# Issuing a head's four cluster-row transfers with the head's first cast instead of its fourth part

## The chip, the cores and the metric

The kernel runs on one core of one Trainium2 chip. The metric is the device time of one execution in microseconds. The core has a matrix engine (TensorE, PE in the rows), VectorE (DVE), ScalarE (ACT), GpSimd (POOL) and SyncE (SP), which here issues nearly all DMA transfers. Each engine works through its own instructions in order and waits on semaphores for the others.

## The reference

Cluster attention, a mixture of experts that sends each token to one expert, and a second dense block. The change lies in the attention:

```
mask = q_assign[:, :, :, None] == k_assign[:, :, None, :]
scores = scale * np.matmul(q, k.transpose(0, 1, 3, 2))
scores = np.where(mask, scores, -1000000000.0)
scores = scores - np.max(scores, axis=-1, keepdims=True)
attn = np.exp(scores)
attn = attn / (np.sum(attn, axis=-1, keepdims=True) + 1e-09)
return np.matmul(attn, v).astype(np.float32)
```

There are 2 x 8 = 16 heads of 768 rows and 64 columns; `q_assign` and `k_assign` are the nearest of 16 centroids by cosine.

## The kernel before, in words

Heads go in pairs `p` (0 to 7), head `h` being half of pair `h // 2`. A head has six row tiles of 128 rows, so the attention is a loop over 96 groups, `g = 6 * h + t`. The order of the instructions on every engine is the order in which the program is written (a manual schedule). One turn of the loop (L1092 to L1114) issues for group `g`: the product of the probabilities with V of an earlier head (`av_step`, L355), the scores of group `g + 2` (`S_mm`, L304 and L319), the transposes of group `g` (`P_T`, L343) with their copies out of PSUM on ACT or DVE (L348, L346), a list of side jobs, the exponential of group `g + 2` on ACT (L330), more side work listed under `after`, and one part of the preparation of a later head.

The scores are two accumulated products. L304 multiplies the tiles `qA` and `kA`, L319 adds `qB` and `kB`, whose rows 0 to 63 are the low parts of a split of q or k and whose rows 64 to 79 are the head's cluster rows: one row per centroid, so that a pair of tokens in different clusters gets a huge negative score. These 16 rows are made for a pair at once (`sims_back`, ACT L230, tile `mk`) and are brought into the operands by `put_mask`: four DMAs of 16 x 384 (24 KB each), two into `qB`, two into `kB`, all issued by SP at L295. The operand tiles have two buffers, so those of head `h` are those of head `h - 2`.

The rest of a head's operands is made by `prep_part(h, i)` in four parts, one in each of the groups `6 * h - 9` to `6 * h - 6`: part 0 a cast of k on ACT (L277), part 1 a second cast (L279) and a subtraction on DVE (L280), part 2 a scaled cast of q (L282), part 3 another (L284) and the DVE's last reading of the pair's raw q (L285). The first L319 of head `h` is issued in group `6 * h - 2`.

What shares SP's queue with L295: `load_raw` (L173 and L174, the raw q and k of a pair, 384 KB each, into two buffers, so the loading of pair `p` waits until the L285 of head `2 * p - 3` is done), `load_v` (L181), the store of finished rows (L394), and a conversion of the last block's 64-bit weights, which runs along with the attention in 16 pieces: `cv_load` (L438, 1024 KB, tile `words`), four steps on ACT and DVE of which the first is ACT's L451, and `cv_store` (L469, 512 KB).

The lines around the change:

```
h2, i2 = divmod(g - 3, NT)
h2 += 2
if 2 <= h2 < NH and i2 < 4:
    prep_part(h2, i2)
    if i2 == 3 and h2 > 2:
        put_mask(h2)
if g == 8:
    put_mask(2)
```

Of the kernel before, what the change touches and what calls it, by code (L numbers as in the profile page):

```python
# [32 lines left out]
def body(ctx, tc, qT, kT, vP, cen, mod, wg, bias, w1, w2, win, wout, out):  # L33
# [121 lines left out]
    def drain():  # L155
        while pend:
            for _ in pend.pop(0):
                pass

    def run(f, *a):  # L160

        drain()
        x = f(*a)
        if hasattr(x, "__next__"):
            next(x, None)
            pend.append(x)
# [101 lines left out]
    def prep_part(h, i):  # L268

        p, o = h // 2, 64 * (h % 2)  # L270
        if i == 0:
            spl[h] = tuple(p_sp.tile([128, S], F32R, tag=n, name=n) for n in ("qA", "kA", "qB", "kB"))
        qA, kA, qB, kB = spl[h]
        q_s, k_s = (r[o:o + 64] for r in raw[p])
        hi, lo = slice(o, o + 64), slice(64 - o, 128 - o)
        if i == 0:
            act.copy(kA[hi], k_s)  # L277
        elif i == 1:
            act.copy(kA[lo], k_s)  # L279
            dve.tensor_tensor(out=kB[0:64], in0=k_s, in1=kA[hi].bitcast(F32), op=ALU.subtract)  # L280
        elif i == 2:
            act.activation(out=qA[hi], in_=q_s, func=AF.Copy, scale=0.125)  # L282
        else:
            act.activation(out=qB[0:64], in_=q_s, func=AF.Copy, scale=0.125)  # L284
            dve.scalar_tensor_tensor(  # L285
                out=qA[lo], in0=q_s, scalar=0.125, in1=qA[hi].bitcast(F32), op0=ALU.mult, op1=ALU.subtract
            )

    def put_mask(h):
        p, i = h // 2, h % 2  # L290
        qA, kA, qB, kB = spl[h]
        for j, x in enumerate((qB, kB)):
            for a in range(2):
                o = 64 * j + 32 * a + 16 * i
                sp.dma_start(  # L295
                    out=x[64:80, a * HS:(a + 1) * HS].bitcast(F32), in_=mks[p][o:o + 16].bitcast(F32)
                )
# [11 lines left out]
    def S_mm(g):  # L309
        if g >= NH * NT:  # L310
            return
        if g not in S_t:
            S_part(g)
        h, t = divmod(g, NT)
        qA, kA, qB, kB = spl[h]
        ps = S_t[g]
        ts = slice(t * 128, t * 128 + 128)
        for i in range(2):
            pe.matmul(ps[:, i, :HS], qB[:80, ts], kB[:80, i * HS:(i + 1) * HS], start=False, stop=True)  # L319
        nm_t[g] = p_m.tile([128, 1], F32, tag="nm", name="nm", bufs=4)  # L320
        dve.tensor_reduce(out=nm_t[g], in_=ps[:, :, :HS], axis=AX.XY, op=ALU.max, negate=True)  # L321

    def S_exp(g):
        if g >= NH * NT:
            return
        h, t = divmod(g, NT)
        if t == 0:
            sums[h] = p_m.tile([128, NT], F32, tag="sums", name="sums", bufs=3)
        P_t[g] = p_P.tile([128, 2, HS], F32, tag="P", name="P")
        act.activation(  # L330
            out=P_t[g], in_=S_t.pop(g)[:, :, :HS], func=AF.Exp, bias=nm_t.pop(g), scale=1.0,
            accum_out=sums[h][:, t:t + 1],
        )

    def P_T(g):
        h, t = divmod(g, NT)
        if t == 0:
            PT[h] = p_PT.tile([128, NT, S], F32, tag="PT", name="PT")
        P = P_t.pop(g)
        for i in range(2):  # L340
            ps = ps_T.tile([128, 3, 128], F32, tag="t", name="Tp")
            for j in range(3):
                pe.transpose(ps[:, j, :], P[:, i, j * 128:(j + 1) * 128], ident)  # L343
            dst = PT[h][:, 3 * i:3 * i + 3, t * 128:(t + 1) * 128]
            if i == 0 and g not in busy:
                dve.tensor_copy(dst, ps)  # L346
            else:
                act.copy(dst, ps)  # L348
# [20 lines left out]
    def av_step(g):  # L369

        h, kt = divmod(g - NT - 1, NT)
        if kt == NT - 1:
            return
        AV(h, kt)
        if kt == NT - 2:
            AV(h, NT - 1)
            fin_av(h)
# [566 lines left out]
    with tc.manual_schedule():  # L944
# [147 lines left out]
        for g in range(NH * NT):  # L1092
            h, t = divmod(g, NT)
            if g > NT:
                av_step(g)
            S_mm(g + 2)
            P_T(g)
            for f, a in jobs.get(g, ()):
                if inspect.isgeneratorfunction(f):
                    run(f, *a)  # L1100
                else:
                    f(*a)
            S_exp(g + 2)
            drain()
            for f, a in after.get(g, ()):
                f(*a)
            h2, i2 = divmod(g - 3, NT)
            h2 += 2
            if 2 <= h2 < NH and i2 < 4:
                prep_part(h2, i2)  # L1110
                if i2 == 3 and h2 > 2:
                    put_mask(h2)
            if g == 8:
                put_mask(2)  # L1114
# [506 lines left out]
```

## Time and profile before

| what | value |
|---|---|
| median of 3 runs | 767.64 us (766.39 to 768.34) |
| the profiled execution, its own time | 767.36 us |
| its span, first to last instruction | 765.6 us |
| mean granted TensorE clock | 0.975 of full speed |
| busy over the span | PE 708.8 us (93%), DVE 450.0 (59%), ACT 416.1 (54%), POOL 128.5 (17%) |

The attention fills about the first 290 us. The times of a row are counted from the span's first instruction. A row that ends in a bracket gives the idle time of its engine just before and what ended it. "SPq" is SP's issuing queue; the time shown there is that of the issue, and the landing of a transfer is a number of its own.

### The profile page before, as it was taken

Reading aid. Unit: us, or ns where it says so; the run is one execution under the profiler, and the core shown is the slowest. Engines: PE = TensorE matmul, PEld = TensorE weight load, DVE = VectorE, ACT = ScalarE, POOL = GpSimd, SP = SyncE. Lnnn points to the kernel's source line nnn. Section 1 sums busy time; section 2 is a strip of 40 time slices with the busy share of each in tenths; the row PEclk is TensorE's granted clock in tenths of the full one; section 3 lists DMA queues with packets and bytes.
Section 4 is the critical chain, followed back from the end, with each engine's and each line's share of the span. In section 5 each row is a group of like instructions: output and inputs, shape, how many; then the busy total and the mean of one; then the engine's idle time right before and its main releaser. Section 6 shows DMA issues by size and latency. Waiting matters only on the chain. (4 is left out here: it accounts for less than half of the span.)

```text
span 765.6 us, 11692 instructions
## 1 busy us (share of the span) xinstructions
PE 708.8 (93%) x4498; PEld 564.4 (74%) x4498; DVE 450.0 (59%) x668; ACT 416.1 (54%) x663; POOL 128.5 (17%) x144
## 2 busy tenths in 40 slices
PE   4997997899798999986999999998999999999998
PEld 2764654556455555874879888997998898999887
DVE  5895987789789975863446563677143233233220
ACT  3886987798779976343446562663323323323310
POOL 4200000000310103635452522252000000000000
PEclk9898999999989999996999999999999999999999
DMA  4314454544553625979967985500010000000000
GB/s 133 105 56 174 145 198 151 171 145 160 183 131 119 199 98 167 236 110 368 355 228 277 345 301 195 179 15 20 10 42 15 28 15 15 15 1 28 1 28 27
DMA packets 38683, 99.28 MB, mean 130 GB/s; under 512 B 8255, under 2 KB 15615, under 8 KB 36577
## 3 DMA queue, kind: packets, MB, share of 16 engines
q1 hardware_dynamic: 35888, 91.42, 36.3%
q0 software_dynamic: 2592, 6.69, 2.4%
q8 instruction: 36, 0.59, 0.3%
q10 hardware_dynamic: 144, 0.39, 0.2%
q14 instruction: 23, 0.18, 0.1%
HBM read 79.13 MB, written 18.28 MB: 127 GB/s over the span
## 5 line engine op out<-in xcount | busy, mean ns | idle before, releaser
L1500 DVE SCALAR_TENSOR_TENSOR sp<-g,sp 128x1024 f32<-128x1024 f32 x24 | 29.4, 1224 | 148.8 <-ACT sp L1499 148.8
L321 DVE TENSOR_REDUCE nm<-S 128x1 f32<-128x768 f32 x96 | 90.9, 948 | 34.3 <-PE S L319 34.0
L1489 PE MATMUL g<-xh,wh 128*128 128x256 f32 x384 | 108.7, 283 | 0.0
L1489 PE MATMUL g<-xh,wl 128*128 128x256 f32 x384 | 107.9, 281 | 0.0
L1489 PE MATMUL g<-xl,wh 128*128 128x256 f32 x384 | 107.9, 281 | 0.0
L1497 ACT ACTIVATE sp<-g 128x1024 f32<-128x1024 f32 x24 | 24.6, 1027 | 136.6 <-PE g L1489 126.7
L330 ACT ACTIVATE P<-S,nm 128x768 f32<-128x768 f32 x96 | 86.9, 905 | 18.9 <-DVE nm L321 16.2
L343 PE MATMUL Tp<-ident,P 128*128 128x128 f32 x576 | 85.6, 284 | 10.7 <-ACT PT L348 7.5
L343 PEld LDWEIGHTS Tp<-ident,P 128*128 128x128 f32 x576 | 68.7, 144 | 24.5 <-ACT PT L348 14.2
L355 PE MATMUL av<-PT,v 128*64 128x384 f32 x384 | 80.7, 517 | 0.0
L741 POOL TENSOR_TENSOR wl<-raw,wh 128x1024 fp32r<-128x1024 f32 x22 | 54.1, 2469 | 139.2 <-ACT wh L740 132.2
L741 DVE TENSOR_TENSOR wl<-raw,wh 128x1024 fp32r<-128x1024 f32 x50 | 65.1, 1343 | 14.5 <-ACT wh L740 14.5
L1489 PEld LDWEIGHTS g<-xl,wh 128*128 128x128 f32 x384 | 73.0, 190 | 0.5
L740 ACT CAST wh<-raw 128x1024 fp32r<-128x1024 f32 x69 | 68.9, 1050 | 8.0 <-DMA raw<-in_w 5.4
L1489 PEld LDWEIGHTS g<-xh,wh 128*128 128x128 f32 x384 | 72.8, 190 | 0.5
L348 ACT COPY PT<-Tp 128x384 f32<-128x384 f32 x144 | 64.0, 477 | 16.8 <-PE Tp L343 16.0
L1489 PEld LDWEIGHTS g<-xh,wl 128*128 128x128 f32 x384 | 73.0, 190 | 0.0
L1524 PE MATMUL o<-wh,gT 128*128 128x512 f32 x216 | 69.7, 394 | 0.0
L319 PE MATMUL S<-kB,qB 80*128 80x384 f32 x192 | 51.8, 353 | 18.0 <-DMA kB<-mk 16.1
L843 PE MATMUL y<-wh,hT 128*128 128x512 f32 x192 | 64.7, 408 | 0.0
L304 PEld LDWEIGHTS S<-kA,qA 128*128 128x128 f32 x192 | 29.7, 194 | 47.1 <-ACT PT L348 16.2
L304 PE MATMUL S<-kA,qA 128*128 128x384 f32 x192 | 60.2, 396 | 1.2 <-ACT P L330 0.9
(284 smaller groups left out, 1396.9 us busy)
## 6 DMA issues: line engine op xcount, KB each, us to landing
raw<-in_w SPq DMA_DIRECT2D x56, 512.0 KB, 7.6
words<-in_win SPq DMA_DIRECT2D x8, 1024.0 KB, 7.4
w_rows<-cvt SPq DMA_DIRECT2D x16, 512.0 KB, 3.0
words<-in_wout SPq DMA_DIRECT2D x8, 1024.0 KB, 5.7
whole<-in_w SPq DMA_DIRECT2D x16, 512.0 KB, 6.2
raw<-w_rows SPq DMA_DIRECT2D x16, 512.0 KB, 4.6
rawq<-in_qT SPq DMA_DIRECT2D x8, 384.0 KB, 3.4
v<-in_vP SPq DMA_DIRECT2D x8, 384.0 KB, 3.4
```

Of the source, the lines that this page charges most:

```text
L304: pe.matmul(ps[:, i, :HS], qA[:, t * 128:t * 128 + 128], kA[:, i * HS:(i + 1) * HS], start=True, stop=False)
L319: pe.matmul(ps[:, i, :HS], qB[:80, ts], kB[:80, i * HS:(i + 1) * HS], start=False, stop=True)
L321: dve.tensor_reduce(out=nm_t[g], in_=ps[:, :, :HS], axis=AX.XY, op=ALU.max, negate=True)
L330: act.activation(out=P_t[g], in_=S_t.pop(g)[:, :, :HS], func=AF.Exp, bias=nm_t.pop(g), scale=1.0, accum_out=sums[h][:, t:t + 1],)
L343: pe.transpose(ps[:, j, :], P[:, i, j * 128:(j + 1) * 128], ident)
L348: act.copy(dst, ps)
L355: pe.matmul(av_t[h][64 * a:64 * a + 64, :], vt[p][:, kt, 64 * i:64 * i + 64], PT[h][:, kt, a * HS:(a + 1) * HS], start=(kt == 0), stop=(kt ...
L740: cp(self.hi, self.raw)
L741: eng.tensor_tensor(out=self.lo, in0=self.raw, in1=self.hi.bitcast(F32), op=ALU.subtract)
L843: pe.matmul(u["y"][j], x, y, start=(kt == 0 and i == 0), stop=(kt == 7 and i == 2))
L1489: pe.matmul(o, a, b[:, kt, :], start=(n == 0 and f % 2 == 0), stop=(n == 11), skip_group_check=True)
L1524: pe.matmul(ys[u][j], x[:, a:a + 128], y, start=(kt == 0 and i == 0), stop=(kt == 15 and i == 2))
```

## The change

`put_mask(h)` for the heads 3 to 15 is called in the turn of part 0 of the head's preparation, three turns earlier. Nothing is computed otherwise, and no instruction is added or removed.

```
-                if i2 == 3 and h2 > 2:
+                if i2 == 0 and h2 > 2:
                     put_mask(h2)
```

The order of instructions on PE, ACT, DVE and POOL is the same before and after. SP's queue changes. Around the loads of pair 3 it reads before (`qB_370` and `kB_371` are head 2's, `qB_566` and `kB_567` head 3's, `qB_747` and `kB_748` head 4's; `mk_419` is pair 1's tile of cluster rows, `mk_715` pair 2's):

```order
L295 DMA qB_370<-mk_419 16x384 x2
L295 DMA kB_371<-mk_419 16x384 x2
L173 DMA rawq_621<-in_qT 128x768
L174 DMA rawk_622<-in_kT 128x768
L438 DMA words_625<-in_win 128x2048
L295 DMA qB_566<-mk_419 16x384 x2
L295 DMA kB_567<-mk_419 16x384 x2
L469 DMA w_rows<-cvt_630 128x1024
L438 DMA words_774<-in_win 128x2048
L181 DMA v_843<-in_vP 128x768
L394 DMA x_rows<-xb_652 128x6x128
L295 DMA qB_747<-mk_715 16x384 x2
```

and now, at the same place:

```order
L295 DMA qB_370<-mk_419 16x384 x2
L295 DMA kB_371<-mk_419 16x384 x2
L295 DMA qB_566<-mk_419 16x384 x2
L295 DMA kB_567<-mk_419 16x384 x2
L173 DMA rawq_625<-in_qT 128x768
L174 DMA rawk_626<-in_kT 128x768
L438 DMA words_629<-in_win 128x2048
L469 DMA w_rows<-cvt_634 128x1024
L295 DMA qB_747<-mk_715 16x384 x2
L295 DMA kB_748<-mk_715 16x384 x2
L438 DMA words_778<-in_win 128x2048
L181 DMA v_847<-in_vP 128x768
```

Head 3's four transfers have moved ahead of the raw q, the raw k and the 1024 KB piece of the weights; head 4's have moved ahead of the next piece, of V and of the store of finished rows. Heads 7 and 8 stand in the same way around the loads of pair 5, heads 11 and 12 around those of pair 7.

Around the loads of pair 4 SP's queue reads before (`qB_936` and `kB_937` are head 5's):

```order
L438 DMA words_928<-in_win 128x2048
L173 DMA rawq_992<-in_qT 128x768
L174 DMA rawk_993<-in_kT 128x768
L469 DMA w_rows<-cvt_907 128x1024
L295 DMA qB_936<-mk_715 16x384 x2
L295 DMA kB_937<-mk_715 16x384 x2
L438 DMA words_1084<-in_win 128x2048
```

and now:

```order
L438 DMA words_928<-in_win 128x2048
L295 DMA qB_936<-mk_715 16x384 x2
L295 DMA kB_937<-mk_715 16x384 x2
L173 DMA rawq_996<-in_qT 128x768
L174 DMA rawk_997<-in_kT 128x768
L469 DMA w_rows<-cvt_907 128x1024
L438 DMA words_1084<-in_win 128x2048
```

Head 5's transfers have moved ahead of the raw q, the raw k and a store of 512 KB; head 9's likewise around the loads of pair 6.

ACT's queue at the first of these places, as it stands now (before, the rows are the same but for the buffers' numbers):

```order
L330 ACTIVATE P_739,sums_593<-S_722,nm_727 128x768
L451 ACTIVATE cvd_742<-words_629 128x1024
L277 CAST kA_746<-rawk_303 64x768
L348 COPY PT_644<-Tp_763 128x3x128
L348 COPY PT_644<-Tp_768 128x3x128
L330 ACTIVATE P_781,sums_780<-S_756,nm_761 128x768
L191 COPY sim_783<-misc_773 128x384
L279 CAST kA_746<-rawk_303 64x768
L362 COPY xTu_793<-av_668 128x384
L348 COPY PT_644<-Tp_805 128x3x128
```

Nothing moved here: the reading of the 1024 KB piece (L451) stands ahead of the two copies (L348) of group 16 and of the exponential (L330) of group 18, head 3's first.

## Rows read from the trace of the kernel before

**Rows 1.** Busy time by stretch: length, engines, then PEclk, DMA share, GB/s.
```profile
70.00:95.00 25.00, 24.31 (x151) 16.48 (x148) 24.06 (x34) 23.52 (x46) 1.01 (x1) 1.00 0.40 132
...
63.00:67.00 4.00, 3.91 (x18) 2.27 (x20) 2.79 (x4) 3.34 (x7) 0.00 (x0) 0.50 0.36 144
...
53.40:62.50 9.10, 5.33 (x32) 3.06 (x30) 5.12 (x7) 5.38 (x12) 0.00 (x0) 0.91 0.85 301
```

**Rows 2.** Waits, 10 to 300 us: total us, times, longest.
```profile
ACT P L330 <- DVE nm L321: 16.2, 20, 2.2
...
PE S L319 <- DMA kB<-mk: 16.1, 5, 5.1
```

**Rows 3.** Timeline of PE at heads 3, 5, 7, 9, 11: start, us, instruction.
```profile
63.09 0.98 PE L319 MATMUL S<-kB,qB 80*128 80x384 f32 x2 [4.35 <-DMA kB<-mk]
...
68.60 0.62 PE L304 MATMUL S<-kA,qA 128*128 128x384 f32 x2
...
97.64 0.58 PE L319 MATMUL S<-kB,qB 80*128 80x384 f32 x2 [1.09 <-DMA kB<-mk]
...
101.04 0.62 PE L304 MATMUL S<-kA,qA 128*128 128x384 f32 x2
...
136.06 0.98 PE L319 MATMUL S<-kB,qB 80*128 80x384 f32 x2 [5.11 <-DMA kB<-mk]
...
140.99 0.62 PE L304 MATMUL S<-kA,qA 128*128 128x384 f32 x2
...
170.24 0.59 PE L319 MATMUL S<-kB,qB 80*128 80x384 f32 x2 [1.32 <-DMA kB<-mk]
...
207.95 1.01 PE L319 MATMUL S<-kB,qB 80*128 80x384 f32 x2 [4.25 <-DMA kB<-mk]
...
214.37 0.64 PE L304 MATMUL S<-kA,qA 128*128 128x384 f32 x2
```

**Rows 4.** Timeline of SP's issues, 53 to 60 us.
```profile
54.25 0.43 SPq L438 DMA_DIRECT2D words<-in_win  x1
54.78 1.25 SPq L295 DMA_DIRECT2D qB<-mk  x2
...
58.28 0.53 SPq L469 DMA_DIRECT2D w_rows<-cvt  x1
58.85 0.43 SPq L438 DMA_DIRECT2D words<-in_win  x1
```

**Rows 5.** Waits of SP's queue, whole span.
```profile
SPq L173 <- DVE qA L285: 62.8, 5, 16.7
```

**Rows 6.** DMA issues, KB, us to landing: 53 to 59.5, then 0 to 300; `words` (min/median/max).
```profile
qB<-mk SPq DMA_DIRECT2D x2, 24.0 KB, 7.7
...
qB<-mk SPq DMA_DIRECT2D x30, 24.0 KB, 2.5
...
DMA to landing us min/median/max: 5.5/5.9/14.0
```

**Rows 7.** Timeline of ACT at heads 3, 7 and 11.
```profile
62.50 1.12 ACT L451 ACTIVATE cvd<-words 128x1024 f32<-128x1024 f32 x1 [3.33 <-DMA words<-in_win]
...
135.41 1.12 ACT L451 ACTIVATE cvd<-words 128x1024 f32<-128x1024 f32 x1 [4.37 <-DMA words<-in_win]
...
207.37 1.12 ACT L451 ACTIVATE cvd<-words 128x1024 f32<-128x1024 f32 x1 [3.75 <-DMA words<-in_wout]
```

**Rows 8.** Waits of ACT, 62.4 to 70.8, 135.3 to 143.2, 207.3 to 216.6 us.
```profile
ACT PT L348 <- PE Tp L343: 1.3, 3, 0.7
ACT xTu L362 <- PE av L355: 0.5, 1, 0.5
...
ACT PT L348 <- PE Tp L343: 1.4, 3, 0.7
...
ACT xTu L362 <- PE av L355: 1.4, 1, 1.4
ACT PT L348 <- PE Tp L343: 1.3, 3, 0.8
```

## The prediction

> **What bounds the kernel now.** I read the busy time by stretch first. Between its disturbances the attention has no single bound: from 70 to 95 us PE, DVE and ACT are each busy 94 to 97% of the time [rows 1], so a wait that stops one of them stops the others soon, and what is given back to one engine counts only as far as the other two can follow. The reader is to keep that in mind for the sum.
>
> Then the waits of the attention by total. The moved transfers appear once, as the wait of PE's L319 for cluster rows that have not landed: 16.1 us in 5 times [rows 2]. PE's timeline places them at the first group of heads 3, 5, 7, 9 and 11: 4.35, 1.09, 5.11, 1.32 and 4.25 us [rows 3]. The heads 4 to 14 of even number, and 13 and 15, show none, although their transfers move as well; moving them removes no wait.
>
> Why only these five? SP's queue answers. Ahead of an odd head's four transfers stands the loading of raw q, which waits for DVE's L285, 62.8 us in 5 times [rows 5]. When it is let go, raw q, raw k and, at heads 3, 7 and 11, a 1024 KB piece of weights go out first; head 3's first transfer is issued at 54.78 [rows 4] and needs 7.7 us to land where the median of all 30 is 2.5 [rows 6]. So the transfers are late because of where they stand: behind 1.8 MB.
>
> The last view is ACT's timeline at the three long waits, and it limits the gain. ACT is held there too, by the piece of weights itself: L451 starts at 62.50, 135.41 and 207.37 after 3.33, 4.37 and 3.75 us of idle time [rows 7], each some 0.6 us before PE gets its cluster rows [rows 3]. The two engines stand still together, for two different transfers of the same queue.
>
> **The change part by part.** *Removed from the place behind the loads:* the wait of L319 at five heads. The four transfers of heads 3, 5, 7, 9, 11 now stand ahead of raw q, are issued seven groups ahead of their use instead of four, and must only wait for PE to be done with the operands of the head two before, whose last L319 stands earlier in the same turn. Seven groups are some 20 us (96 groups in about 275 us), against a landing of 2.5 to 7.7: all five PE waits go, 16.1 us.
>
> *What PE's clock cost after them.* After the long waits the granted clock is 0.50, which is 1.2 of 2.4 GHz, from 63 to 67 us [rows 1]; PE had stood still for 4.35 us. From the restart to the next L304 PE takes 5.51 us at head 3, 4.93 at head 7 and 6.42 at head 11, against 3.40 at head 5 for the same matmuls at full clock [rows 3]: 2.11 + 1.53 + 3.02 = 6.7 us more.
>
> *How much of that ends the program sooner.* At heads 3, 7 and 11 the 1024 KB piece is issued when DVE's L285 lets raw q go, as before, and ACT's L451 stands where it stood. So I let the piece land when it did. At head 3 PE would then go on at 63.09 - 4.35 = 58.74, do the 3.40 us that it has (as at head 5) and one more group's scores, and stop at about 63 for the copies out of PSUM: they stand on ACT behind L451 (1.12 us from 62.50) and the cast L277 (0.8). What is late next is ACT. From L451 on ACT has the same work in the same order; all it can win is the time in which it waited there for PE, restarting late and at half clock: 1.3 + 0.5 us at head 3, 1.4 at head 7, 1.4 + 1.3 at head 11 [rows 8], together 5.9 us. The other end for these three places is the whole PE wait and its clock, 13.7 + 6.7 = 20.4 us, if ACT were not held. I take 5.9, because L451's idle time is there in the rows.
>
> At heads 5 and 9 no piece of weights is read by ACT at that moment; PE, DVE and ACT all wait for the one thing, so the whole 1.09 + 1.32 = 2.4 us comes back. The lower end is nothing, if DVE has no room there.
>
> *Added:* on SP the transfers of the odd heads now stand ahead of raw q, which waits for L285 far longer than they take to issue. Those of heads 4, 8 and 12 hold the next piece of weights back by about the time of four issues (some 2.5 us), and let the 512 KB store go about 1 us sooner than its 58.28 [rows 4]. I price both at nothing: that piece is asked for four groups before ACT reads it, and its usual landing takes 5.9 us [rows 6]. If that cover were gone, ACT would stand for those 2.5 us three times. PE, ACT, DVE and POOL keep their order.
>
> *Not counted:* after each place ACT waits now and then for the row maxima of DVE, 16.2 us in 20 times over the attention [rows 2]. Where DVE comes further ahead than ACT, part of that comes back as well, perhaps 1 us a place. It is in the range.
>
> Sum: 5.9 + 2.4 = 8.3 us. Against the profiled execution's 767.36 us that is **759.1**; the median of the runs shown stands 0.28 us higher, less than they scatter. What comes after the attention starts when it ends, so I let the 8.3 us pass through whole.
>
> **The rivals.** *The whole wait comes back.* ACT's hold could shrink along with PE's if the piece of weights lands sooner. For: between 53.4 and 62.5 us the DMA engines moved 9.1 x 301 = 2.7 MB [rows 1], though only 1.8 MB had been asked for up to that piece, so transfers issued after it took a share before it landed, and of those the next piece now comes later. Against: the masks are only 0.1 MB of it, and the store comes sooner. It would give up to 16.1 + 6.7 = 22.8 us: 744.6. The Trainium skill, "DMA: Bandwidth & Descriptors", section "Anatomy of one DMA", gives a fit of 2.0 us plus the bytes at 436 GB/s, measured on another issuing path. By it, as an estimate, 1.8 MB would be there in 6.2 us after the first load; the case's rows show about 9, and the measurement decides.
>
> *Only the short waits come back.* If ACT or DVE has no use for PE's earlier start at the three held places, 2.4 us remain: 765.0. For: all three engines are near full after it [rows 1]. Against: ACT's waits for PE there are in the rows.
>
> *The position does not matter.* If transfers of one queue finished independently of what stands ahead of them, the late landing would have another cause and go along to the new place; then nothing changes, 767.4. The Trainium skill, same page, section "Queues, rings and completion order", says that completion is not in order of issue; by that rule the 24 KB could overtake the piece. The rows speak against it: 7.7 us behind the loads and 2.5 in the median [rows 6].
>
> *Slower: the piece of weights lands later.* The store of 512 KB now follows the piece without the four issues between them, and transfers behind it do take bandwidth from it (the 2.7 MB above). ACT's hold would then grow at heads 3, 7 and 11. It decides when each hold grows by more than 8.3 / 3 = 2.8 us. The longest landing of such a piece is 14.0 us [rows 6], against about 8.3 at head 3 (54.25 to 62.50), so at most 5.7 us a place: 17.1 - 8.3 = 8.8 us slower, 776.2. Against: the store was in flight during the hold before as well.
>
> **How the numbers follow.** A measurement of this kernel can tell 0.3%, some 2.3 us, from no change. The forecast, ACT-limited, has 0.60; its own range runs from 754.5 (1 to 1.5 us more at each of the three places from DVE's lead or an earlier piece) to 762.1 (the piece 1 us later at each). The whole wait, or much of it, has 0.13, only the short waits 0.12, position without effect 0.09, slower 0.06. The range is 749.0 to 765.2: it takes in the forecast, the short waits, and the nearer part of the full return. Faster is 0.60 + 0.13 + 0.12 = 0.85, same 0.09, slower 0.06.
>
> **What would show it.** Right: no wait of L319 for `qB` or `kB` after head 2; the landing of all 30 `qB` transfers near 2 to 4 us; L451 still idle 3 to 4.5 us for `words` at heads 3, 7 and 11; and PE's wait at these places now in L343, for ACT's L348, about 2 us each and with little or no half clock after it. Wrong: L451's wait gone (then more comes back), or L319's wait back at other heads, or L451's wait grown by 3 us or more.

## The result, and the profile after

The changed kernel takes 759.95 us (758.55 to 760.74, 4 runs), the kernel before 767.1 (766.39 to 768.34, 4 runs): a ratio of 0.9896 [0.9858, 0.9935]. It is faster by about 1%, 7.15 us between the medians. The profiled executions are 760.74 and 767.36 us, 6.6 us apart, and that difference is what the rows below account for.

The waits of the attention, 10 to 300 us (total us, times, longest), of the changed kernel:

```profile
PE Tp L343 <- ACT PT L348: 16.4, 14, 3.0
ACT P L330 <- DVE nm L321: 15.7, 22, 2.3
...
ACT PT L348 <- PE Tp L343: 10.6, 16, 1.8
...
DVE nm L321 <- PE S L319: 9.7, 19, 1.0
ACT cvd L451 <- DMA words<-in_win: 8.6, 2, 4.8
ACT cvd L451 <- DMA words<-in_wout: 6.7, 2, 4.9
```

The wait of L319 for cluster rows, 16.1 us before [rows 2], is gone. What replaced it stands first among the waits of PE, ACT and DVE shown here: PE in L343, for the copies out of PSUM that ACT makes in L348. The last two rows are ACT's L451: it waits four times for its piece of weights, 15.3 us in all, where it waited three times before, 11.45 us [rows 7]. The same view of the kernel before has for L343:

```profile
PE Tp L343 <- ACT PT L348: 7.5, 12, 1.3
```

PE's timeline at head 3, and at the same point of heads 7 and 11 (start, us, instruction, idle time before it):

```profile
58.64 0.52 PE L319 MATMUL S<-kB,qB 80*128 80x384 f32 x2
...
65.31 0.92 PE L343 MATMUL Tp<-ident,P 128*128 128x128 f32 x6 [2.36 <-ACT PT L348]
66.93 0.56 PE L211 MATMUL misc<-ident,sim 128*128 128x128 f32 x3 [0.70 <-ACT sim L191]
67.23 0.90 PE L304 MATMUL S<-kA,qA 128*128 128x384 f32 x2
...
68.67 1.54 PE L343 MATMUL Tp<-ident,P 128*128 128x128 f32 x6
...
135.19 1.28 PE L343 MATMUL Tp<-ident,P 128*128 128x128 f32 x6 [3.03 <-ACT PT L348]
...
205.79 0.92 PE L343 MATMUL Tp<-ident,P 128*128 128x128 f32 x6 [2.94 <-ACT PT L348]
```

Head 3's L319 starts at 58.64 without a wait; before, it started at 63.09 after 4.35 us [rows 3]. PE then works one group further and stops anyway, 2.36 us, because ACT is held. These three waits make 8.33 us where the three of L319 made 13.71.

ACT's timeline, the four starts of L451 that wait:

```profile
63.05 1.12 ACT L451 ACTIVATE cvd<-words 128x1024 f32<-128x1024 f32 x1 [3.79 <-DMA words<-in_win]
...
132.93 1.12 ACT L451 ACTIVATE cvd<-words 128x1024 f32<-128x1024 f32 x1 [4.84 <-DMA words<-in_win]
...
203.53 1.12 ACT L451 ACTIVATE cvd<-words 128x1024 f32<-128x1024 f32 x1 [4.91 <-DMA words<-in_wout]
...
220.03 1.12 ACT L451 ACTIVATE cvd<-words 128x1024 f32<-128x1024 f32 x1 [1.78 <-DMA words<-in_wout]
```

The first three answer to [rows 7], each longer by 0.46, 0.47 and 1.16 us; the fourth, at head 12, is new.

SP's issues at head 3 and at heads 11 and 12:

```profile
41.22 1.14 SPq L295 DMA_DIRECT2D qB<-mk  x2
...
54.32 0.43 SPq L438 DMA_DIRECT2D words<-in_win  x1
57.33 0.33 SPq L469 DMA_DIRECT2D w_rows<-cvt  x1
57.77 1.49 SPq L295 DMA_DIRECT2D qB<-mk  x2
...
60.56 0.58 SPq L438 DMA_DIRECT2D words<-in_win  x1
...
193.92 0.43 SPq L438 DMA_DIRECT2D words<-in_wout  x1
195.25 0.33 SPq L469 DMA_DIRECT2D w_rows<-cvt  x1
196.46 1.96 SPq L295 DMA_DIRECT2D qB<-mk  x2
198.47 1.21 SPq L295 DMA_DIRECT2D kB<-mk  x2
199.73 0.58 SPq L438 DMA_DIRECT2D words<-in_wout  x1
```

Head 3's cluster rows go out at 41.22, 13.6 us sooner than in [rows 4], and land 1.8 us after the issue; before, they landed 5.5 to 7.9 us after it. The piece of weights goes out at 54.32 as before (54.25). Head 4's rows now stand between the store and the next piece: 3.2 us from 57.33 to 60.56, against 0.57 in [rows 4]. At head 12 the same stretch takes 4.5 us, 195.25 to 199.73. The store stands closer behind the piece than before, at head 3 by 1 us (3.0 us against 4.0), at heads 7 and 11 by some 3 us (0.9 and 1.3 against 4.0 and 3.9).

The windows of the changed kernel (length, busy us of PE, PEld, DVE, ACT, POOL, then PEclk, DMA share, GB/s):

```profile
63.00:67.00 4.00, 0.99 (x7) 0.69 (x8) 2.73 (x6) 3.93 (x8) 0.00 (x0) 1.00 0.81 303
...
67.00:70.00 3.00, 3.00 (x13) 2.41 (x13) 2.71 (x3) 2.98 (x7) 0.00 (x0) 0.55 0.06 22
...
137.00:141.00 4.00, 4.00 (x16) 3.25 (x15) 2.60 (x3) 3.98 (x9) 0.00 (x0) 0.50 0.00 2
```

From 63 to 67 ACT is the busy engine, 3.93 of 4 us, and PE stands still for 3 of them: the reverse of [rows 1]. The granted clock still falls once PE has begun again: it is 0.55 in the mean from 67 to 70 us, and 0.50, that is 1.2 of 2.4 GHz, from 137 to 141. At head 7 ACT, now done with its hold, waits for PE soon after (ACT's timeline):

```profile
144.17 0.48 ACT L348 COPY PT<-Tp 128x384 f32<-128x384 f32 x1 [0.95 <-PE Tp L343]
...
146.53 0.48 ACT L348 COPY PT<-Tp 128x384 f32<-128x384 f32 x1 [0.64 <-PE Tp L343]
```

To place the gain I compare when ACT starts the exponential of a group (L330) in two traces. The gain is how much sooner that is than in the kernel before, counted from the group ahead of head 3, since the first 58 us of two executions differ by up to 1.4 us for other reasons. A head's column is taken at its fourth group, `g = 6 * h + 3`; "before head 9" is the last group of head 8.

| gain in us at | head 3 | head 5 | head 7 | before head 9 | head 9 | head 11 | head 12 | end of attention |
|---|---|---|---|---|---|---|---|---|
| changed kernel | 1.72 | 3.04 | 4.05 | 3.60 | 5.11 | 7.55 | 6.59 | 6.58 |
| changed, second trace | 1.68 | 3.00 | 3.84 | 3.21 | 4.72 | 6.74 | 6.75 | 6.74 |
| before, second trace | -0.60 | -0.80 | -0.82 | -0.81 | -0.73 | 1.24 | 1.24 | 1.24 |
| odd heads alone | 4.62 | 5.95 | 6.90 | 6.16 | 7.65 | 10.76 | 10.77 | 10.84 |
| changed, piece first | 5.75 | 7.08 | 13.38 | 13.39 | 14.96 | 22.35 | 22.07 | 22.33 |
| before, piece first | 5.75 | 5.47 | 11.77 | 11.78 | 11.89 | 19.32 | 10.57 | 10.73 |
| odd heads, piece first | 5.75 | 7.09 | 13.33 | 13.36 | 14.90 | 22.32 | 13.16 | 13.38 |
| store later | 1.69 | 3.03 | 3.83 | 3.82 | 5.40 | 8.15 | 8.16 | 8.17 |
| heads 5 and 9 | 0.54 | 1.87 | 1.30 | 1.30 | 2.85 | 2.44 | 2.44 | 2.43 |
| heads 3, 7, 11 | 2.19 | 2.28 | 5.58 | 5.58 | 5.39 | 8.32 | 8.32 | 8.36 |
| scatters later | 2.74 | 4.09 | 7.21 | 7.24 | 8.80 | 10.91 | 10.68 | 5.18 |

The third line shows what such a figure is worth: the same kernel differs from itself by up to 2 us at one long wait. That is head 11, where the second trace has shorter waits and PE needs 5.04 us from its restart to the next L304, not 6.42 as in [rows 3]: the granted clock from 2 to 6 us behind the restart is 0.78 in the mean there, and 0.50 in the first trace. In the changed kernel the gain is 4.41 us at the third group of head 7 and 3.60 before head 9: most of the stretch at half clock and ACT's two waits behind it lie between. The changed kernel's 6.58 us at the end of the attention is the 6.6 us of the whole execution: what follows passes it on.

### The profile page after: what moved, and what is told of

Its sections match the earlier page's. It is cut to its first block, busy times and chain, and to the rows that moved or that the text cites. A ratio compares the mean times of both kernels' runs of the same rounds, so it can differ in the third digit from the quotient of the medians.

```text
span 759.0 us, 11681 instructions
## 1 busy us (share of the span) xinstructions
PE 707.9 (93%) x4498; PEld 565.2 (74%) x4498; DVE 450.5 (59%) x668; ACT 414.4 (55%) x663; POOL 127.6 (17%) x144
## 5 line engine op out<-in xcount | busy, mean ns | idle before, releaser
L343 PE MATMUL Tp<-ident,P 128*128 128x128 f32 x576 | 86.1, 285 | 19.5 <-ACT PT L348 16.4
L330 ACT ACTIVATE P<-S,nm 128x768 f32<-128x768 f32 x96 | 87.0, 907 | 17.6 <-DVE nm L321 15.7
L343 PEld LDWEIGHTS Tp<-ident,P 128*128 128x128 f32 x576 | 68.1, 144 | 34.9 <-ACT PT L348 25.0
L348 ACT COPY PT<-Tp 128x384 f32<-128x384 f32 x144 | 63.8, 479 | 11.4 <-PE Tp L343 10.6
L304 PEld LDWEIGHTS S<-kA,qA 128*128 128x128 f32 x192 | 30.3, 198 | 47.0 <-ACT PT L348 16.7
L304 PE MATMUL S<-kA,qA 128*128 128x384 f32 x192 | 61.3, 402 | 1.2 <-ACT P L330 1.0
L818 PE MATMUL h<-xh,wh 128*128 128x256 f32 x192 | 55.1, 287 | 0.5 <-DVEq L1346 0.5
## 6 DMA issues: line engine op xcount, KB each, us to landing
words<-in_wout SPq DMA_DIRECT2D x8, 1024.0 KB, 20.3
```

Source lines behind the costliest of these rows:

```text
L304: pe.matmul(ps[:, i, :HS], qA[:, t * 128:t * 128 + 128], kA[:, i * HS:(i + 1) * HS], start=True, stop=False)
L330: act.activation(out=P_t[g], in_=S_t.pop(g)[:, :, :HS], func=AF.Exp, bias=nm_t.pop(g), scale=1.0, accum_out=sums[h][:, t:t + 1],)
L818: pe.matmul(o, a, b[:, kt, :], start=(n == 0 and f % 2 == 0), stop=(n == 11), skip_group_check=True)
```

## Experiments

"Piece" below is the 1024 KB of weights that ACT holds for at heads 3, 7 and 11: numbers 1, 6 and 11 of the 16.

**Odd heads alone.** The transfers of even heads stay where they were.

```diff
-                if i2 == 0 and h2 > 2:
+                if i2 == (0 if h2 % 2 else 3) and h2 > 2:
```

> The changed kernel, but only the odd heads' transfers go with the first cast; those of the even heads stay with the fourth part. Theory (only heads 3, 5, 7, 9 and 11 had anything to win): as fast as the changed kernel within 2 us, 758 to 760 us, and no wait of L319 for cluster rows. The wait of ACT's L451 at head 12 (1.78 us in the changed kernel) goes, if it was the even head's four issues that held the piece of weights back. Rival (the even heads' move earns part of the gain): 762 us or more.

757.64 us (757.17 to 758.35), ratio 0.9875 [0.9848, 0.9901]. ACT's timeline:

```profile
61.48 1.16 ACT L451 ACTIVATE cvd<-words 128x1024 f32<-128x1024 f32 x1 [1.02 <-DMA words<-in_win]
...
131.26 1.12 ACT L451 ACTIVATE cvd<-words 128x1024 f32<-128x1024 f32 x1 [4.88 <-DMA words<-in_win]
...
201.51 1.12 ACT L451 ACTIVATE cvd<-words 128x1024 f32<-128x1024 f32 x1 [4.25 <-DMA words<-in_wout]
...
216.13 1.15 ACT L451 ACTIVATE cvd<-words 128x1024 f32<-128x1024 f32 x1
```

No L319 wait for cluster rows is left, so the odd heads carry the whole removal. The wait at head 12 is not there: here the next piece follows the store by 0.37 us (193.89 to 194.26), where the changed kernel lets 4.5 pass. The intervals of the two ratios overlap, so the times don't tell the two kernels apart; in the trace the larger gain (10.84 us) comes mostly from head 3, where this execution's piece took 5.9 us from its issue to ACT's start instead of 8.7, and ACT was held for 1.02 us.

**The piece first.** In its group the piece is asked for ahead of raw q, whose loading waits for L285.

```diff
-            job(g0 - 4, cv_load, j)
+            if j in (1, 6, 11):
+                jobs.setdefault(g0 - 4, []).insert(0, (cv_load, (j,)))
+            else:
+                job(g0 - 4, cv_load, j)
```

With the change:

> The changed kernel, with the 1024 KB piece of weights issued ahead of raw q at heads 3, 7 and 11, so that it no longer waits for DVE's L285. Theory (ACT, held by that piece, keeps back what PE's wait and its half clock cost): ACT's waits for the piece at these heads, 13.5 us in sum, are gone or under 1 us each, and most of the 22.8 us comes back: 744 to 750 us. Rival (all that PE's wait was worth has come back already, the three engines being near full): 758 to 761 us.

745.0 us (744.44 to 745.87), ratio 0.9705 [0.9679, 0.9731]: the fastest of all. The piece goes out before raw q,

```profile
44.94 0.58 SPq L438 DMA_DIRECT2D words<-in_win  x1
54.74 0.33 SPq L173 DMA_DIRECT2D rawq<-in_qT  x1
```

lands after 4.9 us, and L451 waits nowhere. PE's wait for ACT's copies falls back to what it is without a hold, and there is no half clock at head 3 (waits of 10 to 300 us, then a window):

```profile
PE Tp L343 <- ACT PT L348: 7.5, 13, 1.3
```

```profile
63.00:67.00 4.00, 3.81 (x26) 2.93 (x23) 3.92 (x7) 3.95 (x9) 0.00 (x0) 1.00 0.83 340
```

The gain is 22.33 us, close to the 22.8 of the rival in which the whole wait and its clock come back. So it was ACT's hold that kept the change from it.

The same edit to the kernel before:

> The kernel before, its cluster rows in their old place, with the same piece of weights issued ahead of raw q at heads 3, 7 and 11. Theory (the cluster rows were late because of the 1.8 MB ahead of them, and ACT because of the piece): L319 waits 0 to 1.5 us at each of the five heads, as at heads 5 and 9 before, ACT's waits for the piece are gone, no half clock: 748 to 754 us, faster than the changed kernel. Rival (the cluster rows are late whatever stands ahead, by their wait behind L285 alone): waits of 4 us stay at heads 3, 7 and 11, 762 to 767 us.

755.58 us (754.27 to 756.91), ratio 0.9839 [0.9811, 0.9868]: the waits came as the theory has them, the time just above its range. With the piece out of the way the cluster rows behind raw q and raw k are nearly in time (the waits of L319 at head 3 shrink from 4.35 to 0.25 us), and up to head 11 the gain is 19.32 without the change. At head 12 nearly half of that is lost again:

```profile
206.51 0.52 PE L319 MATMUL S<-kB,qB 80*128 80x384 f32 x2
...
217.05 1.01 PE L319 MATMUL S<-kB,qB 80*128 80x384 f32 x2 [8.02 <-DMA kB<-mk]
```

Head 12's rows are issued at 201.66 and need 15 us. In the kernel with both edits they go out at 187.91, ahead of the six scatters of the token list that are the subject further down, and land in 1.9 us. So on top of the piece first the change is worth 3 us up to head 11 and 11.6 at the end. And with the odd heads alone moved:

> The piece of weights ahead of raw q at heads 3, 7 and 11, and only the odd heads' transfers with the first cast. With the piece first and all cluster rows in their old place, head 12's L319 waited 8.0 us for rows that took 15 us to land. Theory (an even head's move is worth something too, once PE comes earlier to its rows: at head 12 every transfer lands late): L319 waits some 8 us at head 12 again, 752 to 755 us. Rival (that wait came from the odd heads' rows being late): no such wait, 744 to 746 us.

755.3 us (754.57 to 756.03), ratio 0.9817 [0.9769, 0.9865], and the same wait:

```profile
215.03 1.01 PE L319 MATMUL S<-kB,qB 80*128 80x384 f32 x2 [8.72 <-DMA kB<-mk]
```

So moving the even heads, which removes no wait by itself, is worth 9 us (22.33 against 13.38) once the attention runs 20 us ahead.

**The store later.** The 512 KB store that follows the piece goes one group later.

```diff
-            after.setdefault(g0 + 4, []).append((cv_store, (j,)))
+            after.setdefault(g0 + (5 if j in (0, 5, 10) else 4), []).append((cv_store, (j,)))
```

> The changed kernel, with the 512 KB store that now follows the piece of weights at heads 3, 7 and 11 issued one group later. ACT's waits for the piece grew by 0.46, 0.47 and 1.16 us and a fourth of 1.78 us appeared. Theory (the store, now directly behind the piece, takes bandwidth from it): the waits go back to some 3.3, 4.4 and 3.8 us and the fourth goes: 757 to 759 us. Rival (something else, such as V's load, which PE now releases sooner): the waits stay as in the changed kernel, 759 to 761 us.

759.02 us (757.52 to 763.21), ratio 0.9898 [0.9854, 0.9943]. The holds are 4.00, 5.39 and 4.59 us, not back at 3.33, 4.37 and 3.75. But the edit changes SP's order at head 3 alone, where the next piece now goes out at 60.65 and the store behind it at 61.2, 5.6 us behind the piece that ACT waits for instead of 3.0. At heads 7 and 11 the order is that of the changed kernel, the store 0.9 and 1.3 us behind the piece. So the theory that the store takes bandwidth from the piece fails at head 3 and is not tested by this run at the other two. The wait at head 12 is gone without a change of order there: the next piece took 14.5 us to land, where it took 20.3 in the changed kernel.

This run also bears on what the half clock costs. At head 7 L451 starts at 134.77 after a longer hold (5.39 us), yet the half clock ends sooner than in the changed kernel, where it is 0.50 from 4 to 8 us behind L451:

```profile
139.00:143.00 4.00, 3.91 (x20) 3.09 (x18) 2.81 (x4) 3.98 (x10) 0.00 (x0) 0.67 0.01 2
```

Here the gain stays, 3.83 at head 7 and 3.82 before head 9, where the changed kernel loses 0.8 us. Its second trace and the run with odd heads alone lose 1.0 and 1.1 at this place.

**The piece alone.** Odd heads alone, the store three groups later and the next piece three groups later, meant to keep everything large from being issued behind the piece before it lands. It does so at head 3 alone; at heads 7 and 11 a store still goes out 0.9 and 1.3 us behind the piece, and only the next piece is gone. This delays other pieces, and the time, 772.91 us in a single execution, says nothing.

```diff
-            job(g0 - 4, cv_load, j)
+            job(g0 - (1 if j in (2, 7, 12) else 4), cv_load, j)
...
-            after.setdefault(g0 + 4, []).append((cv_store, (j,)))
+            after.setdefault(g0 + (7 if j in (0, 5, 10) else 4), []).append((cv_store, (j,)))
```

> Odd heads' transfers with the first cast; at heads 3, 7 and 11 the 512 KB store that follows the piece of weights is issued three groups later and the next piece likewise, so that nothing but raw q, raw k and V shares the queue with the piece. The later pieces are then late themselves, so the time says nothing. Theory (transfers issued behind the piece take bandwidth from it): it starts ACT's L451 7 us or less after its issue, against 8.3 to 8.9 us in the kernel before and 8.7 to 9.6 in the changed one. Rival (the loads ahead of it and its own bytes alone make it so late): 8 us or more.

From its issue to ACT's start the piece takes 7.66 (55.42 to 63.08), 8.70 and 8.77 us. In the kernel before it takes 8.25 (54.25 to 62.50), 8.93 and 8.45. At head 3, the one clean place, 7.66 lies between the theory's 7 and the rival's 8, and within the 5.9 to 8.9 us of the other kernels that issue the piece behind raw q; so what is issued behind the piece is not needed to make it late. Ahead of raw q and raw k, in the run above, it took 4.9 us. What a store close behind adds stays open: at head 7 the piece takes 7.4 to 10.0 us with the store 0.8 to 0.9 us behind it (seven executions) and 8.1 to 8.9 with the store 3 to 4 us behind (three), at head 11 8.8 to 10.0 and 7.8 to 9.5.

**Two heads, and the other three.** Only heads 5 and 9 move, then only heads 3, 7 and 11.

```diff
-                if i2 == 0 and h2 > 2:
+                if i2 == (0 if h2 in (5, 9) else 3) and h2 > 2:
```

> Only the transfers of heads 5 and 9 go with the first cast. Theory (at these two nothing else holds ACT, so that PE's whole wait comes back): PE's waits of 4 to 5 us at heads 3, 7 and 11 stay, those at 5 and 9 go, 2.4 to 3 us faster than before, about 764.5 us. Rival (another engine has no room): within 1 us of before.

765.69 us (764.63 to 769.08, 10 runs), ratio 0.9963 [0.9941, 0.9984]. In the table head 5 gives 1.33 us (0.54 to 1.87) and head 9 1.55 (1.30 to 2.85), where waits of 1.09 and 1.32 us were removed: the whole, as predicted.

```diff
-                if i2 == 0 and h2 > 2:
+                if i2 == (0 if h2 in (3, 7, 11) else 3) and h2 > 2:
```

> Only the transfers of heads 3, 7 and 11 go with the first cast. Theory (ACT, held by the piece of weights, lets only its own waits for PE come back): 4.5 to 6.5 us faster than before, 761 to 763 us; L319 waits 1 to 1.5 us at heads 5 and 9; this and the gain of the run with heads 5 and 9 alone add up to that of the run with all odd heads, within 1.5 us. Rival (the whole wait of PE comes back at the three): 750 us or less.

762.37 us (760.62 to 763.68, 7 runs), ratio 0.9912 [0.9884, 0.994]. The three heads give 2.19, 3.30 and 2.93 us, 8.4 in sum, with holds of 3.50, 2.89 and 4.42 us; the waits at heads 5 and 9 stay, 1.00 and 1.50 us. The smallest hold goes with the largest step. By the medians the gain is 6.3 us, within the forecast of 4.5 to 6.5. In the traces its 8.36 us and the 2.43 of heads 5 and 9 make 10.79, and the run with all odd heads has 10.84: the two parts add up.

**The scatters later.** Head 12's wait falls where six small scatters of the token list run on POOL's queue. They move from group 64 to 72.

```diff
-        job(64, r0_scatter)
+        job(72, r0_scatter)
```

> The changed kernel, with the six scatters of the first batch's token list moved from group 64 to group 72. In every kernel so far a piece of weights issued while they ran took 14 to 20 us to land, and in the changed kernel ACT then waited 1.78 us for it. Theory (the scatters slow the other transfers): the piece issued at some 200 us lands within 10 us, ACT waits for three pieces and not for a fourth, and whatever is issued during the moved scatters lands late in its turn: 757 to 759 us. Rival (the mere number of transfers there): the piece takes 14 us or more again, 759 to 761 us.

763.39 us (758.72 to 767.4, 10 runs), ratio 0.9921 [0.9886, 0.9957], slower than either forecast. POOL's and ACT's timelines:

```profile
216.32 1.20 POOL L589 DMA_INDIRECT token_list<-tokid,ridx  x1 [0.16 <-issue]
...
223.83 2.09 POOL L589 DMA_INDIRECT token_list<-tokid,ridx  x1 [0.23 <-issue]
```

```profile
200.19 1.12 ACT L451 ACTIVATE cvd<-words 128x1024 f32<-128x1024 f32 x1 [5.02 <-DMA words<-in_wout]
215.00 1.15 ACT L451 ACTIVATE cvd<-words 128x1024 f32<-128x1024 f32 x1
...
243.86 1.12 ACT L451 ACTIVATE cvd<-words 128x1024 f32<-128x1024 f32 x1 [3.29 <-DMA words<-in_wout]
```

The wait at head 12 (now 215.00) is gone. The piece issued at 196.62 has all its bytes within 8.4 us, for from 205 us on nothing moves (the last two figures are DMA share and GB/s):

```profile
205.00:209.00 4.00, 4.00 (x18) 2.78 (x17) 3.17 (x7) 4.00 (x10) 0.00 (x0) 0.63 0.00 0
```

Instead the piece that is issued at 225.53, while the last of the moved scatters is under way, lets ACT go only at 243.86, 18.3 us later, and the gain falls from 10.68 to 5.18: 3.3 us are this hold, and the rest comes while PE runs at half clock behind it (0.50 from 246 to 252 us) and ACT waits 1.71 and 1.42 us for PE's L343. The lateness goes where the scatters go: that is shown. How they cause it is not.

**Both kernels again**, one execution each, unchanged, to see how far the holds scatter.

> The kernel before once more, for a second trace. Theory (how long a piece of weights takes to land varies from execution to execution, and the growth of ACT's three waits by 2.1 us in the changed kernel's trace is no part of the change): the three waits differ from 3.33, 4.37 and 3.75 us by up to 1 us or more each. Rival (the landing is fixed by the order of the queue): they agree within 0.2 us.

> The changed kernel once more, for a second trace. Theory (the landing varies from execution to execution): ACT's three waits differ from 3.79, 4.84 and 4.91 us by up to 1 us or more each, and PE's lead over the kernel before at the end of the attention differs from 6.5 us accordingly. Rival (fixed by the order of the queue): they agree within 0.2 us.

Before: 767.08 us, holds of 3.50, 4.32 and 3.10 us. Changed: 762.42 us, holds of 3.66, 5.00 and 5.32, and 0.64 at head 12. In both traces the changed kernel's three holds are 2 to 3 us longer in sum (13.54 and 13.98 against 11.45 and 10.92). One kernel's two traces differ by 0.05 to 0.65 us a hold, less than the theory of both forecasts asks for and mostly within the rival's 0.2, so these two runs do not show that the growth is chance.

## Why the prediction was right, step by step

- *The five waits go.* Right, all of them: head 3's rows, issued 13.6 us sooner, land in 1.8 us, and no wait moved to another head. The landings did not all come "near 2 to 4 us": the median of the `qB` transfers is 3.3, but the rows of five other heads take 5.9 to 7.8 us, and those of head 12 14.1. They are early enough all the same.
- *ACT's hold limits what comes back.* Right, and shown from both sides: with the hold 6.6 us return, without it 22.33.
- *Heads 5 and 9 give all of 2.4.* Right: 1.32 and 1.51 us in the changed kernel, 2.83 in sum, a little more than the waits that went.
- *Heads 3, 7 and 11 give 1.8 + 1.4 + 2.7 = 5.9.* They gave 1.72, 0.56 and 2.44, 4.7 in sum. The mechanism held: ACT's waits for PE behind L451 went (none from 62.4 to 70.8 us, where [rows 8] has 1.8). The size has three errors. I let the piece land when it did, and the holds grew by 0.46, 0.47 and 1.16 us, 2.1 in sum (by 0.33, 0.63 and 1.57 in the second trace). At head 7 the half clock behind the new wait took 0.8 us back (4.41 to 3.60), which the sum does not have. Against these, each place gave 0.4 to 0.9 us beyond ACT's waits, 1.7 in sum, of the size set aside under "Not counted"; whether it comes from DVE's row maxima is not shown. 5.9 - 2.1 - 0.8 + 1.7 = 4.7. What makes the holds grow stays open: a later store did not undo it at head 3, and at heads 7 and 11 no run of the changed kernel sent it later. In the kernel with the scatters moved, which is the changed kernel up to group 64, the holds at heads 3 and 7 are 2.95 and 3.07 us: at these two the growth is no more than executions differ.
- *The moved even heads cost nothing.* Wrong. Its cover was "asked for four groups before ACT reads it, and its usual landing takes 5.9 us", the median of the seven landings out of 16 that the trace has. At head 12 the issues took 4.5 us instead of about 2.5, and the landing took 20.3 instead of 5.9, longer than the 14.0 of [rows 6]. ACT stood for 1.78 us, and the gain fell from 7.55 to 6.59; in the second trace for 0.64 us, at no lasting cost. The other heads' cover held. The store came 1 us closer to the piece at head 3, as said, but some 3 us closer at heads 7 and 11.
- *PE's next wait is L343 for ACT's L348, about 2 us, with little or no half clock.* The place was right, the size 2.36 to 3.03 us, the clock wrong: it was 0.55 from 67 to 70 us and 0.50 from 137 to 141. At head 3 it costs little, since ACT is the engine that is late there: 2.98 of those 3 us busy. At head 7 it lasts longer than ACT's lateness, ACT then waits 0.95 and 0.64 us for PE, and 0.8 us of the gain go.
- *The rivals.* "Position does not matter" falls with the landing of 1.8 us. The whole return was excluded by the hold alone, and came when the hold went. "The piece lands later" did come to pass, at 0.5 to 1.2 us a place, far from the 2.8 at which it decides; that the store behind it is the reason is not shown.

The sum by the table: 4.72 + 2.83 - 0.96 = 6.6 us against the forecast of 8.3. That the whole stands so near is in part luck: errors of both signs cancel, and the hold at head 7 alone differs by 1.9 us (3.07 to 5.00) between executions of what is one program up to there.

By the Trainium skill's rule on completion, weighed in the prediction ("DMA: Bandwidth & Descriptors", "Queues, rings and completion order"), the 24 KB could overtake the loads. Here they did not: head 3's rows took 1.8 us ahead of them and 5.5 to 7.9 behind, and behind they landed at 62.6 to 63.1 us, after ACT had started on the piece at 62.50.

The Trainium skill's fit, measured on another issuing path (same page, "Anatomy of one DMA"), gives, as an estimate, 4.4 us for a piece of 1024 KB that stands alone, and 6.2 for the piece and 768 KB ahead of it. 4.9 was measured where it went ahead of raw q, and 5.9 to 10.0 behind raw q and raw k, 8.7 at head 3 of the changed kernel.

## What to carry to other kernels

A wait that is taken from one engine returns only what the others can use before their own wait ends: look at every engine that stands still at that moment, and for what. Here two transfers on one queue ended 0.6 us apart, and moving the small one alone gave 7 us where moving both ahead of a load whose issue waits gave 22; the large one alone gave 19 up to the place where the queue was slow, and 11 in the end. And a cover must be read where it is needed: a median landing says nothing of the one place at which that queue is slow.

## What was not expected of the hardware

Transfers of SP's queue that are in flight when POOL's six scatters of the token list begin, or are issued while these are under way (198.9 to 220.9 us in the changed kernel), land far later, whatever their size. In the changed kernel, the issues of 195 to 202 us (KB each, median us to landing):

```profile
words<-in_wout SPq DMA_DIRECT2D x1, 1024.0 KB, 20.3
w_rows<-cvt SPq DMA_DIRECT2D x1, 512.0 KB, 15.4
...
qB<-mk SPq DMA_DIRECT2D x2, 24.0 KB, 14.1
kB<-mk SPq DMA_DIRECT2D x2, 24.0 KB, 13.0
token_list<-tokid,ridx POOLq DMA_INDIRECT x3, 14.3
```

The 24 KB take 14.1 us there and 1.8 to 7.8 elsewhere in this trace. It is not the number of bytes: while these transfers are late the DMA engines are busy but move little, 76 GB/s against 305 around the hold of head 3 (DMA share and GB/s at the end of the rows):

```profile
204.00:210.00 6.00, 3.51 (x16) 3.08 (x17) 5.21 (x10) 5.95 (x12) 2.30 (x3) 0.77 0.76 76
60.00:65.00 5.00, 2.95 (x20) 1.14 (x12) 1.00 (x3) 1.96 (x3) 0.00 (x0) 1.00 0.90 305
```

The same stretch gave 15.0 us for head 12's rows in the kernel before with the piece first, and it is why 8 us were lost there. Moving the scatters moved the late piece with them.
